# An attention and mixture kernel: row sums out of the value product, bucket numbers per group of queries, a measured bound of the tokens, and a new written order

## The chip, the cores and the metric

The kernel runs on one core of a Trainium2 chip. Its engines are TensorE (PE, with its weight loads apart as PEld), VectorE (DVE), ScalarE (ACT), GpSimd (POOL) and SyncE (SP), which issues most of the DMAs. Each takes its own instructions in their written order and waits at semaphores for the others. The metric is the time of one execution in microseconds (us) on the device; before the change the median of 3 runs is 1019.14 us (1015.75 to 1021.01).

## The reference

Three steps follow each other. `B`, `H`, `S`, `D` are 2, 8, 768, 64; the 1536 tokens have 512 numbers each.

```python
# attention: a query sees only the keys in its own hash bucket (6 sign bits)
q_bucket = sum_over_bits((q @ proj > 0) * 2**bit);  k_bucket likewise
scores = where(q_bucket == k_bucket, q @ k.T / sqrt(D), -1e9)
attn = exp(scores - max(scores));  attn = attn / (sum(attn) + 1e-9);  x = attn @ v
# 4 experts of 512 -> 1024 -> 512, weighted by normalized domain_probs
x = sum over e of p[:, e] * (relu(x @ w1[e]) @ w2[e])
# one more layer 512 -> 2048 -> 512, with a piecewise quadratic activation
out = g(x @ w_in) @ w_out
```

## The kernel before

All products keep about twice the precision of their operands: an operand is split into a high and a low half ("h", "l"), and three matmuls (high by high, high by low, low by high) take the place of one.

**Attention in units.** A unit is one head and 128 queries, against all 768 keys; there are 96. Twelve groups m of units (three blocks of queries by four pairs of heads) have a preparation `prep(m)` each: q, k and v are loaded, their size is bounded, they are split into halves and transposed by DMA, and the keys' bucket numbers are worked out (`kb`). The first block has the queries of two token tiles (16 units), the second four (32), the third six (48). Unit t then goes through these steps:

- `scores` (PE, L636): four matmuls into a PSUM tile `s` of two banks; two of them have 390 columns, the last six of which are the queries' sign bits, since six columns of projections stand behind the keys.
- `q_bucket` (DVE, L646): six bits to a bucket number, with a sum over the six.
- `mask` (DVE, L652): -2**80 where the key's bucket is another. It needs the bucket number.
- `row_max` (DVE, L658): mask added, the result to the tile `e` (three buffers), with the row's minimum.
- `norm` (ACT, L666): the minimum plus 9.704, that is 14 powers of two.
- `expo` (ACT, L671): exp in place, with the row's sum as a second output.
- `p_hi` (ACT, L678), `p_lo` (DVE or POOL, L686, in pieces): the two halves `pn`.
- `p_t` (SP, L691): both are transposed by DMA into `pt`.
- `rsum` (DVE, L696 for each unit, L698 for two units at once): one over (sum plus a small number) times a scale.
- `av`, five units later (PE, L706, L707 and L709, 18 matmuls of 64 columns): the product with the values. From the 17th unit on it is written into free columns of the PSUM tile `s` that the unit five later uses for its scores.
- `comb` (ACT, L716): times the reciprocal, into the token's row of `acc`.

There are two PSUM tiles `s`, so the scores of unit t+2 wait until the tile is read out: by `row_max` of unit t and by `comb` of unit t-5.

**Filling work.** The first token tiles are ready when the 16th unit is combined. Then jobs of the experts run in TensorE's gaps: `JOBS_A`, 19 jobs of 256 tokens by 512 hidden columns each. A job has 48 matmuls of 256 columns (L850 to L852) and 24 of 512 (L868 to L870). ACT writes the high half of weights (L832) and of the hidden layer (L857), DVE or POOL the low halves (L836, L862), and DVE adds the results to `acc` (L880). Before the first job each of two tiles is transposed (L779). Where nothing is to do, unneeded matmuls of zeros (L1040) are written into TensorE's list.

**The order** of all this is fixed when the kernel is built. A planner (`Order`) gets every step with the engines that may do it, a cost, what it reads and writes, and a key. It goes through the steps as a list: of those that can start first it takes the one of the smallest key. The keys are times in units plus a table of numbers (`K_LD` to `K_L2`). Where a step may run on two engines, the planner's costs choose.

**Second phase.** What follows (`step`, `l1b`, `l2b`) is written by hand: the rest of the experts and the last layer, in 16-bit halves. There tokens are scaled by a power of two, bounded in `x_bound` (L1261 to L1267) from the sizes of v.

Of the kernel before, what the change touches and what calls it, by code (L numbers as in the profile page):

```python
# [19 lines left out]
NB = 6  # L20
# [5 lines left out]
LSHIFT = 9.70406052783923  # L26
EPS = 1e-9 * 2.0 ** 14
# [259 lines left out]
def attn_moe_kernel(ctx: ExitStack, tc, q, k, v, proj, probs, w1, w2, w_in, w_out, out):  # L287
# [23 lines left out]
    const.tile([128, 80], F32, name="pad")  # L311
# [20 lines left out]
            vs=kv_p.tile([128, 2, 6, 128], F16, name=f"vs{p}"),  # L332
# [54 lines left out]
    def all_max(nm, n, src, key, r, use, e_out, s_out, w_e, w_s, tag="mx"):  # L387

        st, gb, gc, bm = {}, S.bank(), S.bank(), S.buf(tag, 4)

        def f1():
            st["mx"] = sm_p.tile([4, 1], F32, tag=tag, name=tag)
            st["dg"] = sm_p.tile([4, 4], BF16, tag="d" + tag, name="d" + tag)
            dve.tensor_reduce(st["mx"][0:n], gb.ps[0:n, 0:128], AX.X, ALU.max)
# [25 lines left out]
    sw_b = const.tile([128, 2], F32, name="sw_b")  # L420
    ekv = [const.tile([128, 3], F32, name=f"ekv{i}") for i in range(8)]
    skv = [const.tile([128, 3], F32, name=f"skv{i}") for i in range(8)]

    def prep(m):
# [158 lines left out]
        for i in range(2):  # L583
            tk(f"sw{m}{i}", dict(dve=0.07 + 0.067 * n, sp=0.55), lambda e, i=i: q_swap(i, e), max(t - Q_SW[g], dh + 1.5), r=[f"xq{m}"], w=[f"yq{m}{i}"],
               use=[bxq], port=True, dma=(0.46, 0.75, 0.12 * n, 2.5))
        if kv:
            dv = t - V_HI[g]
            tk(f"vhi{m}", dict(act=0.83), lambda e: hi_(vs[:, :, :, 0:64], st["rv"], 1), dv, r=[vt, f"s{m}.1"] + va, w=[f"vsh{p}"], use=bv)
            tk(f"vlo{m}", dict(dve=0.93), lambda e: lo_(vs[:, :, :, 64:128], vs[:, :, :, 0:64], st["rv"], 1), dv + 0.4,
# [27 lines left out]
    K_LD, V_LD, Q_LD = (17.214, -0.655, 23.922), (12.706, 49.119, 26.44), (12.617, -7.397, 30.338)  # L617
    K_AB, V_AB, Q_AB = (49.192, 45.359, 12.84), (11.282, -23.228, 13.919), (13.718, 15.385, -1.48)
    K_HI, V_HI, Q_HI = (32.317, -13.974, 10.395), (7.816, 1.17, -30.115), (14.167, 8.304, 9.444)
    K_M = 1.18  # L620
    K_NA = 0.604
    K_BI, Q_SW = (2.317, -33.361, 20.951), (10.382, -5.64, -40.487)
# [7 lines left out]
    def scores(t):  # L630
        m, hh, c = units[t]
        st = P[m]
        sps = s_tile(t)
        for j, n in ((1, 390), (0, 384)):
            for i in range(2):
                pe.matmul(sps[:, j, 0:n], st["xq"][1 - i][:, hh * QG[pgs[m][0]][2] + c], st["x"][:, hh, 384 * j:384 * j + n],  # L636
                          start=(i == 0), stop=(i == 1))

    def q_bucket(t):
        u = U[t]  # L640
        if "sm2" not in u:
            s2 = sm_p.tile([128, 6, 2], F32, tag="usm", bufs=6, name="usm")
            U[t ^ 1]["sm2"] = u["sm2"] = s2
        sm = u["sm"] = u["sm2"][:, :, t % 2]
        junk = sm_p.tile([128, NB], F32, tag="junk", bufs=2, name="junk")
        dve.scalar_tensor_tensor(junk, u["s"][:, 1, 384:390], 0.0, pow6, ALU.is_gt, ALU.mult, accum_out=sm[:, 0:1])  # L646

    def mask(t):
# [3 lines left out]
        dve.tensor_scalar(mk, P[m]["kb"][:, hh], u["sm"][:, 0:1], -BIG, ALU.not_equal, ALU.mult)  # L652

    def row_max(t):
        m, hh, c = units[t]
        u = U[t]
        e = u["e"] = e_p.tile([128, 768], F32, tag="e", name="e")
# [35 lines left out]
    def rsum(t, i):  # L693
        s2 = U[t]["sm2"]
        if i < 2:
            dve.tensor_scalar(s2[:, 4, i:i + 1], s2[:, 3, i:i + 1], EPS, P[units[t][0]]["kvs"][:, 1:2], ALU.add, ALU.mult)  # L696
        else:
            dve.reciprocal(s2[:, 5], s2[:, 4])  # L698

    def av(t, gb):  # L700
# [3 lines left out]
        o = u["av"] = s_tile(t + AVL + 1)[:, 0, 384:448] if gb is None else gb.ps[:, 0:64]  # L704
        for i in range(6):
            pe.matmul(o, u["pt"][:, i], vs[:, hh, i, 0:64], start=(i == 0), stop=False)  # L706
            pe.matmul(o, u["pt"][:, i], vs[:, hh, i, 64:128], start=False, stop=False)  # L707
        for i in range(6):
            pe.matmul(o, u["pt"][:, 6 + i], vs[:, hh, i, 0:64], start=False, stop=(i == 5))  # L709

    def comb(t):
# [11 lines left out]
    def unit(t):  # L723
# [17 lines left out]
        if on:  # L741
# [3 lines left out]
            kvm = m - 4 if pgs[m][0] == 1 else m  # L745
# [3 lines left out]
            tk(f"sc{t}", dict(pe=0.66), lambda e: scores(t), t - 1 + K_SC, r=[f"xq{m}", f"yq{m}0", f"yq{m}1", f"x{p}{hh}", "xk6"], after=["bits01"] if t == 0 else [],  # L749
               w=[f"sco{t}"], use=[bS[t], st["bxq"]], excl=ex)  # L750
            tk(f"qb{t}", dict(dve=0.075), lambda e: q_bucket(t), t, r=[f"sco{t}"], w=[f"sm0.{t}"], use=[bS[t], bU[t]], excl=ex, tick=t)
            tk(f"mk{t}", dict(dve=0.329), lambda e: mask(t), t + 0.05, r=[f"sm0.{t}", f"kb{p}{hh}0", f"kb{p}{hh}1"], w=[f"mk{t}"], use=[bmk, bU[t]], port=True)
            tk(f"rm{t}", dict(dve=0.94), lambda e: row_max(t), t + 0.1, r=[f"sco{t}", f"mk{t}", f"sc{m}"], w=[f"e{t}", f"sm1.{t}"],
               use=[be, bS[t], bmk, st["bsc"], bU[t]], excl=ex)
            tk(f"nm{t}", dict(act=0.095), lambda e: norm(t), t + 0.2, r=[f"sm1.{t}"], w=[f"sm2.{t}"], use=[bU[t]])
# [742 lines left out]
```

## Time and profile before

The profiled execution took 1019.93 us, and the span from its first to its last instruction is 1018.1 us.

| | before |
|---|---|
| median of 3 runs | 1019.14 us |
| profiled execution, its span | 1019.93 us, 1018.1 us |
| busy: PE, PEld | 963.4 us (95%), 619.1 us (61%) |
| busy: DVE, ACT, POOL | 731.4 us (72%), 732.2 us (72%), 353.8 us (35%) |
| mean granted clock of TensorE | 0.979 of full speed |
| DMA | 121.51 MB, mean 119 GB/s |

Three stretches are to be told apart. Up to 89 us there are attention units and preparations only. Then, until the first matmul of the second phase at 430.66 us, units and jobs share the engines. The rest is the second phase. Busy time of an engine counts each instruction from its start to its end. TensorE's matmuls overlap, and small instructions on DVE and ACT overlap the next by some 0.07 us; what one costs its engine is therefore read from the distance between two starts.

### The profile page before, as it was taken

How to read it: one execution, taken by the hardware profiler on the slowest of the kernel's cores; microseconds unless marked ns; L12 is line 12 of the kernel's file. 1: busy time of each engine (PE TensorE's matmuls, PEld its weight loads, DVE VectorE, ACT ScalarE, POOL GpSimd, SP SyncE). 2: the span in 40 equal slices, each digit the busy share in tenths (PEclk: the TensorE clock that was granted, in tenths of full speed). 3: DMA queues.
4: the chain of work that ended last, by engine and by line, in shares of the span. 5: the costliest groups of instructions: out<-in, count | busy, mean ns of one | idle time of the engine just before them, and what ended most of it. 6: DMA issues, size and time to landing. Idle time of an engine off the chain costs nothing.

```text
span 1018.1 us, 19428 instructions
## 1 busy us (share of the span) xinstructions
PE 963.4 (95%) x6874; PEld 619.1 (61%) x6874; DVE 731.4 (72%) x1946; ACT 732.2 (72%) x1590; POOL 353.8 (35%) x382
## 2 busy tenths in 40 slices
PE   6668999989999999999999999999998999999998
PEld 2347777868787888875555555555544555555553
DVE  6899978898887886446666657565577678774654
ACT  6888978888887877348776777667776785656442
POOL 0433545544554545515110111104242353434221
PEclk7789999999999999999999999999999999999999
DMA  8899999998999977261434333110110111100002
GB/s 227 191 204 197 199 239 217 251 211 165 233 191 177 195 160 161 81 220 42 146 88 141 103 111 118 42 42 22 43 42 21 43 42 43 41 1 1 1 36 90
DMA packets 254836, 121.51 MB, mean 119 GB/s; under 512 B 180753, under 2 KB 239505, under 8 KB 254737
## 3 DMA queue, kind: packets, MB, share of 16 engines
q1 hardware_dynamic: 251904, 117.89, 49.4%
q10 hardware_dynamic: 2832, 2.36, 0.8%
q8 instruction: 54, 0.88, 0.4%
q14 instruction: 46, 0.37, 0.1%
HBM read 70.28 MB, written 3.15 MB: 72 GB/s over the span
## 4 chain that ended last, share of the span: by engine, by line
PE 62%; DVE 14%; ACT 10%; DMA 9%; issue 4%; SPq 1%; POOL 1%; DVEq 0%; ACTq 0%; POOLq 0%
PE mm L1334 7%; PE mm L1335 7%; PE mm L1336 7%; PE o L1370 6%; PE o L1372 6%; PE o L1371 6%; DMA raw<-in_moe_w_dram 5%; PE s L636 3%; DVE hl L1358 2%; PE m L868 2%; PE m L850 2%; PE m L870 2%; PE m L851 2%; PE m L869 2%; PE m L852 2%
## 5 line engine op out<-in xcount | busy, mean ns | idle before, releaser
L686 POOL TENSOR_TENSOR pn<-e,pn 128x192 f16<-128x192 f32 (+3 forms) x146 | 127.3, 877 | 185.0 <-DVE pn L686 56.6
L1353 POOL TENSOR_TENSOR gg<-gg,ga 128x384 f32<-128x384 f32 x64 | 71.0, 1109 | 153.0 <-DVE ga L1352 142.6
L1343 DVE TENSOR_TENSOR hl<-gg,hh 128x384 f16<-128x384 f32 x72 | 42.9, 595 | 81.3 <-ACT hh L1342 81.1
L658 DVE CUSTOM_DVE_ANT_0 e<-s,mk,sc 128x768 f32<-128x768 f32 x96 | 96.7, 1009 | 3.8 <-ACT acc L716 2.2
L850 PE MATMUL m<-x0h,w1h 128*128 128x256 f32 x304 | 92.1, 303 | 1.1 <-DVE acc L880 1.1
L1350 ACT ACTIVATE ga<-mm,half,k 128x384 f32<-128x384 f32 x64 | 42.7, 667 | 67.9 <-PE mm L1336 46.7
L636 PE MATMUL s<-xk,xq 128*128 128x384 f16 (+1 forms) x384 | 82.4, 340 | 9.1 <-DVE usm L658 7.6
L671 ACT ACTIVATE e<-e,usm 128x768 f32<-128x768 f32 x96 | 89.3, 930 | 2.5
L851 PE MATMUL m<-x0l,w1h 128*128 128x256 f32 x304 | 86.3, 284 | 0.1
L852 PE MATMUL m<-x0h,w1l 128*128 128x256 f32 x304 | 86.1, 283 | 0.0
L678 ACT ACTIVATE pn<-e 128x768 f16<-128x768 f32 (+3 forms) x118 | 84.3, 715 | 2.2 <-DMA pt<-pn 1.3
L1352 DVE SCALAR_TENSOR_TENSOR ga<-ga 128x384 f32<-128x384 f32 x64 | 38.4, 601 | 63.8 <-ACT ga L1350 63.8
L1372 PE MATMUL o<-w2l,hl 128*128 128x512 f16 x216 | 81.9, 379 | 1.1 <-DVE hl L1358 1.1
L1370 PE MATMUL o<-w2l,hh 128*128 128x512 f16 x216 | 82.0, 380 | 0.0
L1371 PE MATMUL o<-w2l,hh 128*128 128x512 f16 x216 | 81.9, 379 | 0.0
L1358 DVE SCALAR_TENSOR_TENSOR hl<-gg,k,hh 128x384 f16<-128x384 f32 x64 | 58.4, 913 | 20.3 <-ACT hh L1357 20.0
L1370 PE MATMUL o<-w2h,hh 128*128 128x512 f16 x192 | 72.9, 380 | 0.0
L1371 PE MATMUL o<-w2h,hh 128*128 128x512 f16 x192 | 72.8, 379 | 0.0
L1372 PE MATMUL o<-w2h,hl 128*128 128x512 f16 x192 | 72.8, 379 | 0.0
L1372 PEld LDWEIGHTS <-hl 128*128 128x128 f16 x408 | 39.9, 98 | 49.7 <-DVE hl L1358 1.6
L1341 ACT ACTIVATE gg<-mm 128x384 f32<-128x384 f32 x72 | 34.8, 483 | 45.1 <-PE mm L1104 20.9
L868 PE MATMUL m<-w2h,hh 128*128 128x512 f32 x152 | 64.6, 425 | 0.7 <-DVE hl L862 0.7
(258 smaller groups left out, 2953.1 us busy)
## 6 DMA issues: line engine op xcount, KB each, us to landing
raw<-in_moe_w_dram SPq DMA_DIRECT2D x127, 256.0 KB, 3.5
r<-in_moe_w_in_dram SPq DMA_DIRECT2D x16, 512.0 KB, 3.6
r<-in_moe_w_out_dram SPq DMA_DIRECT2D x16, 512.0 KB, 3.6
rawx<-in_moe_w_dram SPq DMA_DIRECT2D x24, 256.0 KB, 4.4
out_dram<-acc SPq DMA_DIRECT2D x12, 256.0 KB, 2.0
raw<-in_moe_w_dram ACTq DMA_DIRECT2D x9, 256.0 KB, 3.5
w<-in_moe_w_dram SPq DMA_DIRECT2D x8, 256.0 KB, 6.2
rk<-in_k_dram SPq DMA_DIRECT2D x5, 384.0 KB, 4.1
```

The source lines that it names most:

```text
L636: pe.matmul(sps[:, j, 0:n], st["xq"][1 - i][:, hh * QG[pgs[m][0]][2] + c], st["x"][:, hh, 384 * j:384 * j + n], start=(i == 0), stop=(i == 1))
L658: dve.tensor_tensor_reduce(out=e.rearrange("p (a b) -> p a b", a=2), in0=u["s"][:, :, 0:384], in1=u["mk"].rearrange("p (a b) -> p a b", a= ...
L671: act.activation(u["e"], u["e"], AF.Exp, scale=-1.0, bias=sm[:, 2:3], accum_out=sm[:, 3:4])
L678: act.activation(u["pn"][:, c0:c1], u["e"][:, c0:c1], AF.Copy)
L686: eng[e].tensor_tensor(u["pn"][:, 768 + c0:768 + c1], u["e"][:, c0:c1], u["pn"][:, c0:c1], ALU.subtract)
L850: pe.matmul(ps[:, 0:n], hi[:, ws], xh[:, kc, xs], start=(kc == 0), stop=False)
L851: pe.matmul(ps[:, 0:n], hi[:, ws], xl[:, kc, xs], start=False, stop=False)
L852: pe.matmul(ps[:, 0:n], lo[:, ws], xh[:, kc, xs], start=False, stop=(kc == KC - 1))
L868: pe.matmul(o, hh[:, ts], whi, start=(f == 0), stop=False)
L1370: pe.matmul(o, hh[:, ts], whi, start=(f == 0), stop=False)
L1371: pe.matmul(o, hh[:, ts], wlo, start=False, stop=False)
L1372: pe.matmul(o, hl[:, ts], whi, start=False, stop=(f == 3))
```

## The change

- A column of ones is put beside the values, so `av` gives the row sum as a 65th column; exp no longer sums. `rsum` is now done after `av`, for each unit, out of PSUM. `comb` may run on DVE as well as ACT.
- The bias of exp is the row minimum itself; `norm` goes.
- The queries' bits are no longer columns of the scores. For each group a step `q_bits` makes them with two matmuls of 6 columns for each unit of the group, and two DVE instructions make all bucket numbers of the group. `mask` then needs no scores.
- The tokens' bound of the second phase is measured: a sum of absolute values over each of the 12 tiles of `acc` (DVE or ACT), a maximum, and the chain that other bounds have too. `x_bound` goes.
- The table of numbers is another, so the planner writes another order.

```diff
@@ prep
+        def q_bits():
+            for i in range(2 * n):
+                for z in range(2):
+                    pe.matmul(gq.ps[:, NB * i:NB * i + NB], st["xq"][1 - z][:, i], x[:, i // n, 768:774], start=(z == 0), stop=(z == 1))
+        def q_bucket(i):
+            if i == 0:
+                st["jq"] = sm_p.tile([128, 12, NB], F32, tag="jq", bufs=1, name="jq")
+                dve.scalar_tensor_tensor(st["jq"][:, 0:2 * n], gq.ps[...], 0.0, pow6..., ALU.is_gt, ALU.mult)
+            else:
+                st["qb"] = sm_p.tile([128, 12], F32, tag="qb", bufs=2, name="qb")
+                dve.tensor_reduce(st["qb"][:, 0:2 * n], st["jq"][:, 0:2 * n], AX.X, ALU.add)
+        tk(f"qbp{m}", dict(pe=0.12 * n), lambda e: q_bits(), dq, r=[f"xq{m}", f"yq{m}0", f"yq{m}1", "xk6"], w=[f"qbp{m}"], use=[bxq], grp=gq)
...
@@ table of numbers (two of its lines)
-    K_AV, K_SC, K_CB, K_HI_, K_LO_ = -10.443, -1.424, 0.486, 1.113, 2.995
+    K_AV, K_SC, K_CB, K_HI_, K_LO_ = -101.924, 32.319, 1.164, -27.484, 2.38
@@ a unit
-        for j, n in ((1, 390), (0, 384)):
+        for j in (1, 0):
-        dve.scalar_tensor_tensor(junk, u["s"][:, 1, 384:390], 0.0, pow6, ALU.is_gt, ALU.mult, accum_out=sm[:, 0:1])
-        dve.tensor_scalar(mk, P[m]["kb"][:, hh], u["sm"][:, 0:1], -BIG, ALU.not_equal, ALU.mult)
+        dve.tensor_scalar(mk, P[m]["kb"][:, hh], P[m]["qb"][:, i:i + 1], -BIG, ALU.not_equal, ALU.mult)
-        act.activation(sm[:, 2:3], sm[:, 1:2], AF.Copy, bias=LSHIFT)
-        act.activation(u["e"], u["e"], AF.Exp, scale=-1.0, bias=sm[:, 2:3], accum_out=sm[:, 3:4])
+        act.activation(u["e"], u["e"], AF.Exp, scale=-1.0, bias=u["sm"][:, 0:1])
-            dve.tensor_scalar(s2[:, 4, i:i + 1], s2[:, 3, i:i + 1], EPS, P[units[t][0]]["kvs"][:, 1:2], ALU.add, ALU.mult)
-            dve.reciprocal(s2[:, 5], s2[:, 4])
+            dve.tensor_scalar(sm[:, 1:2], u["av"][:, 64:65], EPS, P[units[t][0]]["kvs"][:, 1:2], ALU.add, ALU.mult)
+            dve.reciprocal(sm[:, 2:3], sm[:, 1:2])
-            pe.matmul(o, u["pt"][:, i], vs[:, hh, i, 0:64], start=(i == 0), stop=False)
+            pe.matmul(o, u["pt"][:, i], vs[:, hh, i, 0:65], start=(i == 0), stop=False)
-        act.activation(acc[TT0[g] + c][:, hd * 64:hd * 64 + 64], u["av"], AF.Copy, scale=u["sm"][:, 5:6])
+        if e == "act":
+            act.activation(to, u["av"][:, 0:64], AF.Copy, scale=sc)
+        else:
+            dve.tensor_scalar(to, u["av"][:, 0:64], sc, None, ALU.mult)
...
-            tk(f"cb{a}", dict(act=0.2), lambda e: comb(a), a + da + K_CB, r=[f"av{a}", f"sm5.{a // 2}"], w=a_of(tt), grp=gb,
+            tk(f"rs{a}", dict(dve=0.12), lambda e: rsum(a, 0), a + da + K_CB - 0.2, r=[f"av{a}", f"s{kvm}.1"], w=[f"sm4.{a}"], grp=gb, **ub)
+            tk(f"rr{a}", dict(dve=0.08), lambda e: rsum(a, 1), a + da + K_CB - 0.1, r=[f"sm4.{a}"], w=[f"sm5.{a}"], use=[bU[a]])
+            tk(f"cb{a}", dict(act=0.2, dve=0.15), lambda e: comb(a, e), a + da + K_CB, r=[f"av{a}", f"sm5.{a}"], w=a_of(tt), grp=gb, **ub)
@@ bound of the tokens
+        def x_scan(e, tt):
+            if e == "dve":
+                dve.tensor_reduce(am_x[:, tt:tt + 1], acc[tt], AX.X, ALU.add, apply_absolute_value=True)
+            else:
+                junk = nat_p.tile([128, 768], BF16, tag="ja", name="ja")[:, 0:512]
+                act.activation(junk, acc[tt], AF.Abs, accum_out=am_x[:, tt:tt + 1])
...
-            dve.tensor_tensor(e, v[0], v[1], ALU.add)
-            ...
-        for b in range(2):
-            x_bound(b)
+        dve.tensor_scalar(exk, ex, 2.0 ** 15, None, ALU.mult)
```

In the written order of the changed kernel 69 of the 96 combinations stand on DVE and 27 on ACT; before all 96 stood on ACT. The low halves of `pn` are 45 pieces on DVE (before 87) and 160 on POOL (before 146, smaller ones). Of the 12 scans of tokens 8 stand on DVE, and 28 weight loads are issued on ACT's queue (before 9).

On DVE, around the `row_max` of the 62nd unit, this stood before (`junk` is the bits times powers of two, `usm` a unit's small numbers, `mk` the mask, `pn` and `w2l` low halves):

```order
L646 SCALAR_TENSOR_TENSOR junk,usm<-s,pow_109 128x6
L836 TENSOR_TENSOR w2l<-raw_3825,w2h 128x256
L652 TENSOR_SCALAR mk<-kb_124,usm 128x768
L686 TENSOR_TENSOR pn<-e,pn 128x192
L836 TENSOR_TENSOR w2l<-raw_3836,w2h 128x256
L658 ISA e,usm<-s,mk,sc 128x768
L658 ISA usm 128x1
L696 TENSOR_SCALAR usm<-usm,skv_149 128x1
```

Around the same `row_max` this stands now (`qb` holds the group's bucket numbers):

```order
L717 TENSOR_SCALAR usm<-s,skv_152 128x1
L683 ISA e,usm<-s,mk,sc 128x768
L683 ISA usm 128x1
L719 RECIPROCAL usm<-usm 128x1
L533 TENSOR_SCALAR sc<-sc 128x1
L741 TENSOR_SCALAR acc<-s,usm 128x64
```

The test of bits is gone from between the scores and the mask. A first instruction of `rsum` that reads `av`'s columns of the tile `s` stands ahead of `row_max`, and reciprocal and combination stand behind it.

On ACT, around the exp of the same unit, this stood before (`hh` is the hidden layer's high half, `w2h` that of weights):

```order
L666 ACTIVATE usm<-usm 128x1
L820 DMA raw_4804<-in_moe_w_dram 128x512
L832 ACTIVATE w2h<-raw_4742 128x512
L671 ACTIVATE e,usm<-e,usm 128x768
L857 ACTIVATE hh<-m 128x256
L678 ACTIVATE pn<-e 128x768
```

And now, from the next exp on:

```order
L691 ACTIVATE e<-e,usm 128x768
L854 ACTIVATE w1h<-raw_4793 128x512
L879 ACTIVATE hh<-m 128x256
L698 ACTIVATE pn<-e 128x768
L838 DMA raw_5216<-in_moe_w_dram 128x4x128
```

The step `norm` no longer stands ahead of exp, and exp writes `e` alone.

On PE, where the queries of a new group (the last pair of heads, third block) come in, scores were followed by a job's matmuls:

```order
L636 LDWEIGHTS xq_5462
L636 MATMUL s<-xk_129,xq_5462 128x390
L636 LDWEIGHTS xq_5461
L636 MATMUL s<-xk_129,xq_5461 128x390
L636 LDWEIGHTS xq_5462
L636 MATMUL s<-xk_129,xq_5462 128x384
L636 LDWEIGHTS xq_5461
L636 MATMUL s<-xk_129,xq_5461 128x384
L868 MATMUL m<-w2h,hh 128x512
```

Now 24 pairs like the last two follow the scores of the unit before (`xq_5801`, `xq_5802` are the new group's queries):

```order
L661 LDWEIGHTS xq_4992
L661 MATMUL s<-xk_126,xq_4992 128x384
L594 LDWEIGHTS xq_5802
L594 MATMUL m<-xk_129,xq_5802 128x6
L594 LDWEIGHTS xq_5801
L594 MATMUL m<-xk_129,xq_5801 128x6
```

The two wide matmuls lose six columns, and each pair of narrow ones brings a weight load of its own. There are 192 narrow matmuls in all, 32 of them for the first block.

## Rows read from the trace of the kernel before

**Rows 1.** Windows: PE, PEld, DVE, ACT, POOL busy (instructions), PEclk, DMA share, GB/s.

```profile
0.00:89.00 89.00, 61.50 (x519) 33.85 (x520) 75.36 (x305) 71.92 (x169) 21.40 (x29) 0.81 0.92 207
89.00:430.60 341.60, 329.33 (x3233) 274.76 (x3231) 279.19 (x868) 272.43 (x646) 169.39 (x211) 1.00 0.92 191
442.00:1018.10 576.10, 563.78 (x3068) 301.86 (x3066) 372.40 (x757) 385.28 (x770) 158.69 (x136) 1.00 0.19 59
```

**Rows 2.** PE's groups, 89 to 430.6 us: count | busy, mean ns | idle before.

```profile
L850 PE MATMUL m<-x0h,w1h 128*128 128x256 f32 x304 | 92.1, 303 | 1.1 <-DVE acc L880 1.1
...
L868 PE MATMUL m<-w2h,hh 128*128 128x512 f32 x152 | 64.6, 425 | 0.7 <-DVE hl L862 0.7
L636 PE MATMUL s<-xk,xq 128*128 128x390 f16 (+1 forms) x300 | 62.2, 330 | 0.0
...
L706 PE MATMUL s<-vs,pt 128*128 128x64 f16 x450 | 37.4, 195 | 5.4 <-DMA pt<-pn 3.3 <-DVE usm L696 1.6 <-DVE junk L646 0.5
```

**Rows 3.** PE in order of time: start, us, line, what, count.

```profile
203.09 0.39 PE L870 MATMUL m<-w2h,hl 128*128 128x512 f32 x1
203.32 0.20 PE L706 MATMUL s<-vs,pt 128*128 128x64 f16 x1
...
203.68 0.34 PE L709 MATMUL s<-vs,pt 128*128 128x64 f16 x6
```

**Rows 4.** The same, a job's first layer a little later.

```profile
205.19 0.28 PE L850 MATMUL m<-x0h,w1h 128*128 128x256 f32 x1
205.31 0.28 PE L851 MATMUL m<-x0l,w1h 128*128 128x256 f32 x1
```

**Rows 5.** The chain of waits, scores of one unit: start, us.

```profile
111.48 0.66 PE s L636 x4
```

**Rows 6.** What PE waited for, 89 to 430.6 us: total, times, longest.

```profile
PE s L706 <- DMA pt<-pn: 3.3, 6, 1.5
PE m L597 <- DMA xk<-nk: 2.2, 3, 1.3
```

**Rows 7.** The first token tile's transposes on PE.

```profile
89.04 0.60 PE L779 MATMUL m<-ident,acc 128*128 128x128 f32 x4
```

**Rows 8.** ACT in order of time, one unit.

```profile
68.87 0.19 ACT L666 ACTIVATE usm<-usm 128x1 f32<-128x1 f32 x1
68.96 0.31 ACT L716 ACTIVATE acc<-m,usm 128x64 f32<-128x64 f32 x1
69.16 0.93 ACT L671 ACTIVATE e<-e,usm 128x768 f32<-128x768 f32 x1
70.00 0.18 ACT L671 ACTIVATION_READ_ACCUMULATOR e<-e,usm 128x1 f32 x1
70.09 0.47 ACT L613 ACTIVATE kb<-m 128x384 bf16<-128x384 f32 x1
```

**Rows 9.** DVE in order of time, one unit.

```profile
203.55 0.20 DVE L696 TENSOR_SCALAR usm<-usm,skv 128x1 f32<-128x1 f32 x1
203.67 0.15 DVE L646 SCALAR_TENSOR_TENSOR junk<-s,pow 128x6 f32<-128x6 f32 x1
...
203.79 0.17 DVE L698 RECIPROCAL usm<-usm 128x2 f32<-128x2 f32 x1
203.87 0.82 DVE L652 TENSOR_SCALAR mk<-kb,usm 128x768 bf16<-128x768 bf16 x1
```

**Rows 10.** DVE's groups by form, 0 to 430.6 us.

```profile
L686 DVE TENSOR_TENSOR pn<-e,pn 128x192 f16<-128x192 f32 x71 | 28.9, 408 | 0.0
...
L824 DVE TENSOR_REDUCE am_w<-raw 128x1 f32<-128x512 f32 x5 | 3.3, 680 | 3.4 <-DMA raw<-in_moe_w_dram 3.3
```

**Rows 11.** PE around a single narrow matmul.

```profile
415.56 0.17 PE L411 MATMUL m<-dmxw,ones 2*128 2x2 bf16 x1
415.66 0.50 PE L868 MATMUL m<-w2h,hh 128*128 128x512 f32 x1
```

**Rows 12.** ACT at the start of the second phase.

```profile
434.89 0.63 ACT L832 ACTIVATE w2h<-raw 128x512 fp32r<-128x512 f32 x1 [0.81 <-DMA raw<-in_moe_w_dram]
```

More of the change, by code (lines that the diff above doesn't have):

```diff
@@ L310, in attn_moe_kernel @@
     ident = const.tile([128, 128], F32, name="ident")
-    const.tile([128, 80], F32, name="pad")
+    const.tile([128, 24], F32, name="pad")
     half = const.tile([128, 1], F32, name="half")
@@ L331, in attn_moe_kernel @@
             kb=kv_p.tile([128, 2, 768], BF16, name=f"kb{p}"),
-            vs=kv_p.tile([128, 2, 6, 128], F16, name=f"vs{p}"),
+            vs=kv_p.tile([128, 1568], F16, name=f"vs{p}")[:, 0:1560].rearrange("p (h c d) -> p h c d", h=2, c=6),
         )
@@ L420, in attn_moe_kernel @@
     sw_b = const.tile([128, 2], F32, name="sw_b")
+    am_x = const.tile([128, 12], F32, name="am_x")
+    mx_x = const.tile([128, 2], F32, name="mx_x")
+    ex = const.tile([128, 2], F32, name="ex")
+    sx = const.tile([128, 2], F32, name="sx")
     ekv = [const.tile([128, 3], F32, name=f"ekv{i}") for i in range(8)]
@@ L656, in row_max @@
         u = U[t]
+        sums(t)
         e = u["e"] = e_p.tile([128, 768], F32, tag="e", name="e")
@@ L951, in fill @@
                    r=[f"l2.{j}.{i}.3", "pr"], w=a_of(tt), grp=gb)
-    K_LDW, K_WHI, K_WLO, K_XT = 2.992, -0.836, -3.345, 20.559
-    K_EVA, K_EVD, K_L2 = 0.084, -7.646, -32.852
+        for tt in range(6, 12):
+            x_bound(tt)
+        tk("mxx", dict(dve=0.15), lambda e: dve.tensor_reduce(mx_x, am_x.rearrange("p (b t) -> p b t", b=2), AX.X, ALU.max), 100,
+           r=[f"amx{i}" for i in range(12)], w=["mxx"])
+        all_max("mxy", 2, lambda: mx_x, 100, ["mxx"], [], lambda: ex, lambda: sx, ["ex"], ["sx"], "mxv")
+    K_XS = -79.736
+    K_LDW, K_WHI, K_WLO, K_XT = -227.274, -8.417, -22.583, -52.671
+    K_EVA, K_EVD, K_L2 = -8.736, -15.304, -25.186
     with tc.manual_schedule():
@@ L966, in attn_moe_kernel @@
             dve.memset(pow6[:, i:i + 1], float(2 ** i))
+        for x in kvs:
+            pool.memset(x["vs"][:, :, :, 64:65], 1.0)
         make_identity(nc, ident)
@@ L1250, in need @@
                     next(w64)
-        ex = const.tile([128, 2], F32, name="ex")
-        sx = const.tile([128, 2], F32, name="sx")
         exk = const.tile([128, 2], F32, name="exk")
@@ L1257, in attn_moe_kernel @@
         prk, k5 = {}, {}
-        def x_bound(b):
-            e, v = ex[:, b:b + 1], [ekv[4 * b + i][:, 1:2] for i in range(4)]
-            dve.tensor_tensor(e, v[0], v[1], ALU.add)
-            dve.tensor_tensor(e, e, v[2], ALU.add)
-            dve.tensor_tensor(e, e, v[3], ALU.add)
-            dve.tensor_scalar(e, e, 4.0, None, ALU.mult)
-            pow2(e)
-            dve.reciprocal(sx[:, b:b + 1], e)
-            dve.tensor_scalar(exk[:, b:b + 1], e, 2.0 ** 15, None, ALU.mult)
         def x_f16(kc, c0, c1):
```

82 lines of the change are left out of this document (43 added, 39 removed).

## The prediction

> **What bounds the kernel now.** I read three views in this order: the windows, to find the stretches with different limits; TensorE's groups and its order in time, for how full its list really is; and its waits.
>
> The windows split the span in three [rows 1]. After 442 us the second phase keeps PE busy for 563.8 of 576.1 us, and the change touches only one DVE step at its start. In the first 89 us PE is busy for 61.5 us, DVE for 75.4 and ACT for 71.9, at a granted clock of 0.81: here the units alone run, and DVE and ACT hand work to each other. This ends when the 16th unit is combined and the first tile's transposes start [rows 7]. From then to 430.6 us PE shows 329.3 of 341.6 us [rows 1]. That busy time counts overlaps, so I add up its list by distances between starts. A matmul of 256 columns takes 0.12 us [rows 4], one of 512 takes 0.23, one of the value product 0.03 (12 starts in 0.36 us) [rows 3], a unit's four scores 0.66 [rows 5]. The counts in this stretch [rows 2] give 3 x 304 x 0.12 = 109.4, 3 x 152 x 0.23 = 104.9, 75 x 0.66 = 49.5, and 81 units of the value product (75 into `s`, 6 elsewhere) x 18 x 0.03 = 43.7 us, together 307.5. The small groups (bucket bits of keys, transposes, filler) add some 15 us, an estimate. So PE's list fills about 322 of 341.6 us, and 19 us are gaps. PE is the bound here, and an engine that gets less work shortens this stretch only by what it takes out of those 19 us. The longest named waits are for the transposed halves (3.3 us) and for transposed keys (2.2 us) [rows 6]; both are DMAs that the change leaves as they are.
>
> So there are three places to win or lose: the first 89 us, PE's list, and PE's gaps.
>
> **The first 89 us.** Up to the first tile's high half, the written order of ACT had 20 `norm`, 19 sums out of exp and 15 combinations; now it has none of the first two and 3 combinations. By distances between starts a `norm` costs 0.09, a sum 0.09 and a combination 0.20 us [rows 8], so 1.8 + 1.7 + 2.4 = 5.9 us go. But one more exp (0.84) and three more sums for preparations of later groups (0.74 each by exp's neighbours) now stand ahead of that point, some 3 us. On DVE 21 bit tests at 0.12 us go [rows 9] (2.5 us), and 8 fewer low-half pieces of about 0.4 us [rows 10] (some 4 us). In return 12 combinations come (1.8 us at 0.15, since no row shows a 64-column one on DVE: it lies between the 0.12 of a small instruction [rows 9] and the 0.33 of one of 192 columns [rows 10]), 12 bucket instructions (1.2), 7 more reciprocals at 0.08 [rows 9], three more copies of queries, one scan, and one more mask and `row_max` (1.3). That leaves about 1 us less. So this stretch gains 1 us if DVE's list decides and 5.9 if ACT's does and the work drawn ahead finds gaps. I take 4, since each unit's chain also loses two steps on ACT between the minimum and the end of exp. For the range I keep a loss of 1 (the later groups' sums delay the first tile) and a gain of 8 (the 5.9, and 2 more if the 79 filler matmuls that stand ahead of the 12th unit's end, before 48, keep the clock up).
>
> **PE's list.** 160 of the 192 narrow matmuls stand after the first block, where PE is full. No row shows a matmul of 6 columns with a full weight load of its own. The nearest is the value product, which has such a load for 64 columns and takes 0.03 us [rows 3]: 160 x 0.03 = 4.8 us. From above, the distance of a lone 2-column matmul to the next is 0.10 us [rows 11], which makes 16 us; from below, if all fall into gaps, nothing. I take 4.8, because they stand in a row of pairs as those of rows 3 do. Six fewer columns in 192 scores and one more in two thirds of the value product are each about half a microsecond and cancel. The 32 narrow ones of the first block have PE's gaps there as cover.
>
> The Trainium skill ("TensorE: Matmul & The Clock Gate", section "Back-to-back issue gap") says that a stream of weight load and matmul pairs is paced by both and sustains about 81 ns per matmul at 128 columns. By it the 160 pairs would cost 13.0 us. The value product's pairs at 30 ns [rows 3] speak against it here; it is the fifth case below.
>
> **PE's gaps.** Over all units ACT loses 96 x (0.09 + 0.09) and 69 combinations x 0.20 [rows 8], 31 us, and gets four scans and 19 DMA issues, some 4 us: it is relieved by about 27 of 344 us [rows 1]. DVE is hardly relieved: 96 tests (11.5 us) and 42 low-half pieces (some 14 us) go, while 69 combinations (10.4), 48 more reciprocals (3.8), 24 bucket instructions (3.6), eight scans at 0.6 [rows 10] (4.8) and seven copies come, so about 1 us less of 354 [rows 1]. POOL takes over the low halves, some 23 us more of 191 [rows 1], and is half idle. What moves is the balance: before the last scores stood 774 first-layer and 381 second-layer matmuls in units of one of the three lines each, now 714 and 336, so attention runs ahead and 60 x 0.12 + 45 x 0.23 = 17.6 us of jobs more follow it, where PE has nothing to wait for but weights. I take 8 of the 19 us of gaps as won; the bounds are nothing (the gaps are DMA's [rows 6]) and 17.
>
> The scans of tokens and their chain are in these sums. The 14 instructions of `x_bound` lay beside matmuls, so their going gains nothing, and what is late there stays: ACT is held by a weight load [rows 12], and the same rows stand in the same order in the changed kernel.
>
> **A wait that is added.** `rsum` now waits on DVE for the value product, which waits for a transpose. Queued behind it are `row_max`, the next mask and low halves; exp waits for the first. The combination, two more DVE steps later, frees the PSUM tile for scores. I price this at nothing in the sum: a tile is used every second unit, that is each 2 x 341.6 / 75 = 9.1 us [rows 1, 2], and PE's scores had no idle time ahead of them in this stretch [rows 2].
>
> **Sum.** 1019.9 (the profiled execution) - 4 + 4.8 - 8 = 1012.7. The median of the runs shown is 0.8 lower, so I predict 1012 us.
>
> **Rivals.**
> - *Forecast*, chance 0.48: 1012, own range 1007 to 1018 (first stretch -1 to -6, gaps -4 to -12).
> - *Relief where nobody waits*, 0.27: the first 89 us gain 4, the list grows by 4.8, and the gaps stay, since they belong to DMAs and to DVE, which is as loaded as before: 1020.7, as a median 1020. For it: rows 6 and DVE's sum. Against it: ACT's 27 us.
> - *The new order closes the gaps*, 0.14: -8 + 4.8 - 17 = -20.2, as a median 999. For it: 13.6 us in which DVE was idle in the first 89 us [rows 1]. Against it: no edit shortens a DMA.
> - *The longer way out of PSUM*, 0.06, slower: `rsum`, a `row_max` of some 0.9 us, a reciprocal and the combination now stand between the value product and the release of `s`, where one ACT instruction of 0.3 us stood [rows 8]. It frees about 1 us later. If PE stands still for that at every fourth of 75 units, 19 us come on top of the forecast: 1031. It decides from the point at which scores follow the release by less than 1 us. Against it: the 9.1 us of a tile's round.
> - *Pairs at 81 ns*, 0.05: 1012 + 160 x 0.051 = 1020, a rival by the rule that the skill's page gives above.
>
> **How the numbers follow.** About 0.5% (5.1 us) is what a measurement of this kernel can tell from no change, so faster is below 1014.0 and slower above 1024.2. The forecast's case gives 0.34 faster and 0.14 same, the second 0.02, 0.22 and 0.03, the third 0.14 faster, the fourth 0.06 slower, the fifth 0.04 same and 0.01 slower: 0.50, 0.40 and 0.10. The range 1000 to 1024 leaves out half of the third case, the fourth, and the upper ends of the second and fifth, some 0.17.
>
> **What would show it.** The first tile's transposes start at about 85 us. The narrow matmuls follow each other at 0.03 us. The first matmul of the second phase starts at about 423 us (430.7 before), and the second phase lasts as long as before. PE's gaps between these points shrink from some 19 to 11 us. The forecast is wrong if the transposes start no earlier than 88 us, if PE waits for the combination ahead of scores, or if POOL's low halves come so late that PE waits for transposed halves for more than the 3.3 us of before.

## The result, and the profile after

The changed kernel is slower: a median of 1029.91 us (4 runs, 1028.64 to 1032.05) beside 1018.74 for the kernel before on the same chip, a ratio of 1.0108 with a 95% interval of 1.0086 to 1.0129. The prediction was 1012, with a range of 1000 to 1024: the measured time lies 18 us above the one and 6 above the other. The profiled execution took 1028.64 us (span 1026.8); the one of before took 1019.93 (span 1018.1). These 8.7 us can be placed by three points in the two traces:

| start of | before | after | added in the stretch |
|---|---|---|---|
| the first tile's transposes | 89.0 | 91.2 | +2.2 |
| the first matmul of the second phase | 430.7 | 437.9 | +5.0 |
| the end | 1018.1 | 1026.8 | +1.5 |

The windows of the changed kernel's trace, cut at these points (columns as in [rows 1]):

```profile
0.00:91.20 91.20, 67.77 (x638) 40.45 (x638) 76.59 (x296) 69.92 (x126) 28.28 (x41) 0.91 0.96 207
91.20:437.90 346.70, 334.76 (x3339) 279.83 (x3335) 280.51 (x807) 243.47 (x424) 181.97 (x215) 0.99 0.92 185
450.00:1026.80 576.80, 563.44 (x3065) 301.42 (x3063) 373.79 (x757) 385.09 (x770) 157.54 (x136) 1.00 0.19 59
```

ACT lost 29 us in the middle stretch (243.5 for 272.4 [rows 1]) and 2 in the first, a little more than the 27 that the prediction counted; DVE stayed as it was and POOL took over some work. Yet the stretch is longer. The DMA share, the last but one number, is the one that hasn't moved: 0.92 in the middle, before and after. It stands in [rows 1] as well. (It adds up the time of all packets over 16 engines, and packets overlap: over the first 330 us of the changed kernel it comes to 1.02. So 1 is not a strict ceiling.)

The groups of PE in the middle stretch answer to [rows 2]:

```profile
L872 PE MATMUL m<-x0h,w1h 128*128 128x256 f32 x304 | 92.4, 304 | 0.0
L890 PE MATMUL m<-w2h,hh 128*128 128x512 f32 x152 | 65.8, 433 | 0.3 <-DVE acc L902 0.3
...
L727 PE MATMUL s<-vs,pt 128*128 128x65 f16 x450 | 39.2, 196 | 4.3 <-DMA pt<-pn 2.3 <-DVE usm L717 1.9
L728 PE MATMUL s<-vs,pt 128*128 128x64 f16 x450 | 38.6, 194 | 0.0
L594 PE MATMUL m<-xk,xq 128*128 128x6 f16 x128 | 4.1, 166 | 2.2 <-DMA xq<-xq 2.2
```

The same count of job matmuls is there, and the narrow ones (L594) are new. Mean durations overlap, so the cost is again read from starts. One value product and one group of narrow matmuls, in order of time:

```profile
114.13 0.54 PE L594 MATMUL m<-xk,xq 128*128 128x6 f16 x16 [0.40 <-DMA xq<-xq]
114.53 0.48 PE L890 MATMUL m<-w2h,hh 128*128 128x512 f32 x1
...
204.92 0.20 PE L727 MATMUL s<-vs,pt 128*128 128x65 f16 x1
204.96 0.20 PE L728 MATMUL s<-vs,pt 128*128 128x64 f16 x1
...
205.31 0.34 PE L730 MATMUL s<-vs,pt 128*128 128x65 f16 x6
```

Sixteen narrow pairs go in 0.40 us, 0.025 each. The first twelve starts of a value product take 0.39 us; in [rows 3] they took 0.36. What PE waited for in the middle stretch (us in total, times, longest), beside [rows 6]:

```profile
PE m L621 <- DMA xk<-nk: 2.4, 1, 2.4
PE s L727 <- DMA pt<-pn: 2.3, 3, 0.9
PE m L594 <- DMA xq<-xq: 2.2, 2, 1.8
PE s L727 <- DVE usm L717: 1.9, 1, 1.9
```

The longest waits are DMAs again. That of L594 is new: the narrow matmuls wait for a copy of the queries. The one for `rsum` (L717) is hardly longer than it was (1.6 us [rows 2]).

TensorE's granted clock has a part in this. Behind the 1.8 us wait of L594, at 188 us, it is at 0.5 of full speed (1.2 GHz) from 191.4 to 194.8 us, and the starts of 256-column matmuls stand 0.21 us apart instead of 0.12:

```profile
191.22 0.40 PE L872 MATMUL m<-x0h,w1h 128*128 128x256 f32 x1
191.43 0.41 PE L873 MATMUL m<-x0l,w1h 128*128 128x256 f32 x1
```

The middle stretch has a second such fall of 3.4 us at 222 us, behind a wait for `kb` at 220; before the change it had one, at 156 us. An estimate from these rows: one more fall costs at most half of its 3.4 us, 1.7 of the 5.0 us that the stretch grew by.

I then took every distance between two starts of PE and set what exceeds the usual distance of its kind (its shape and that of the matmul ahead of it) by more than 0.12 us apart as a gap. From the first tile's transposes to the second phase the gaps are 16.1 us before and 15.9 after: not one of the 8 us that I took is won. The list is longer by about 5. In the first phase as a whole it gained 5.0 us of narrow matmuls, 3.0 of value products (53.7 to 56.7), and 4.5 of zeros, most of which fill gaps of the first 91 us.

### The profile page after: what moved, and what is told of

The parts are those of the page before. It is cut to its first block, busy times and chain, and to the rows that moved or that the text cites. A ratio compares the mean times of both kernels' runs of the same rounds, so it can differ in the third digit from the quotient of the medians.

```text
span 1026.8 us, 19476 instructions
## 1 busy us (share of the span) xinstructions
PE 975.1 (95%) x7095; PEld 630.7 (61%) x7095; DVE 732.5 (71%) x1863; ACT 701.0 (68%) x1325; POOL 372.0 (36%) x396
## 2 busy tenths in 40 slices
DMA packets 254432, 120.89 MB, mean 118 GB/s; under 512 B 180673, under 2 KB 239169, under 8 KB 254337
## 3 DMA queue, kind: packets, MB, share of 16 engines
HBM read 70.28 MB, written 3.15 MB: 72 GB/s over the span
## 4 chain that ended last, share of the span: by engine, by line
PE 65%; DVE 12%; ACT 9%; DMA 8%; issue 3%; POOL 1%; SPq 1%; ACTq 0%; POOLq 0%; DVEq 0%
PE mm L1365 7%; PE mm L1366 7%; PE mm L1367 7%; PE o L1401 6%; PE o L1403 6%; PE o L1402 6%; PE s L661 4%; PE m L872 3%; PE m L873 3%; PE m L874 3%; DMA raw<-in_moe_w_dram 3%; PE m L890 2%; PE m L891 2%; PE m L892 2%; DVE hl L1389 2%
## 5 line engine op out<-in xcount | busy, mean ns | idle before, releaser
L706 POOL TENSOR_TENSOR pn<-e,pn 128x192 f16<-128x192 f32 (+3 forms) x160 | 150.2, 945 | 188.9 <-DVE mk L676 31.6
L661 PE MATMUL s<-xk,xq 128*128 128x384 f16 x384 | 80.7, 334 | 7.1 <-DVE usm L683 4.2
L873 PE MATMUL m<-x0l,w1h 128*128 128x256 f32 x304 | 86.5, 284 | 0.0
L698 ACT ACTIVATE pn<-e 128x768 f16<-128x768 f32 (+3 forms) x104 | 81.0, 787 | 5.9 <-DMA pt<-pn 1.9
```

What stands on the lines that cost most here:

```text
L661: pe.matmul(sps[:, j, 0:384], st["xq"][1 - i][:, hh * QG[pgs[m][0]][2] + c], st["x"][:, hh, 384 * j:384 * j + 384], start=(i == 0), stop=( ...
L698: act.activation(u["pn"][:, c0:c1], u["e"][:, c0:c1], AF.Copy)
L706: eng[e].tensor_tensor(u["pn"][:, 768 + c0:768 + c1], u["e"][:, c0:c1], u["pn"][:, c0:c1], ALU.subtract)
L873: pe.matmul(ps[:, 0:n], hi[:, ws], xl[:, kc, xs], start=False, stop=False)
```

## The experiments

Each ratio is against runs of the kernel before on the same chip, with its 95% interval. "Theory A" is that the change adds to TensorE's list and that its gaps are not ACT's or DVE's; the others are named where they come up. Differences in us are between medians. Unless it is said, the instructions of each engine stand in the same order as in the kernel that was edited, so only their cost differs.

**Relief alone.** The kernel before, without `norm`:

```
 def norm(t):
-    act.activation(sm[:, 2:3], sm[:, 1:2], AF.Copy, bias=LSHIFT)
+    return
```

> The kernel before with the 96 norm steps on ACT left out (exp takes the row minimum itself as its bias), every other instruction in the same place on its engine. One part of the change alone, the one that only removes. Rival C and the prediction (ACT's relief closes TensorE's gaps and shortens the first 89 us): 96 x 0.09 = 8.6 us less on ACT and one step less in each unit's chain, -3 to -5 us, 0.995 to 0.997. Theory A (the gaps are not ACT's): within 1 us, 0.999 to 1.001.

Measured 1.0009 (0.9984 to 1.0035). The same with the bucket tests taken off DVE as well (`mask` compares with `pow6[:, 0:1]`):

> The kernel before without the 96 norm steps on ACT and without the 96 bucket tests on DVE (the mask compares with a constant instead, so the masks are not the reference's), every other instruction in its place. ACT loses 8.6 us and DVE 11.5, more than the whole change relieves DVE by. The prediction's mechanism (relief closes gaps): -6 to -10 us, 0.990 to 0.994. Theory A with D (list, fixed pieces and DMAs): within 2 us, 0.998 to 1.001.

Measured 1.0003 (0.9982 to 1.0025). Its windows, cut at the same two points:

```profile
0.00:87.20 87.20, 60.43 (x519) 34.51 (x520) 73.51 (x261) 69.92 (x149) 21.85 (x29) 0.86 0.92 210
87.20:430.00 342.80, 329.67 (x3233) 276.15 (x3231) 274.30 (x720) 263.78 (x570) 170.23 (x211) 0.99 0.92 191
```

The first tile comes 1.8 us earlier (87.2 for 89.0), and the middle stretch gives back most of it (342.8 for 341.6). Twenty us less of work on ACT and DVE are worth nothing that can be measured, at most 0.2% by the intervals. ACT is relieved here by 8.6 us and not by the 31 of the change, DVE by 11.5; for this much the main term of the prediction is settled: the gaps weren't ACT's or DVE's.

**Whose gaps are they?** The changed kernel with transposes of half the size:

```
-sp.dma_start_transpose(out=u["pt"], in_=u["pn"])
+sp.dma_start_transpose(out=u["pt"][:, 0:6], in_=u["pn"][:, 0:768])
...
-pe.matmul(o, u["pt"][:, 6 + i], vs[:, hh, i, 0:65], ...)
+pe.matmul(o, u["pt"][:, i], vs[:, hh, i, 0:65], ...)
```

> The changed kernel with the transposes of probabilities on the high halves alone (6 pieces instead of 12; the value product takes the high half a second time, so TensorE's list is the same). It leaves the low halves of the probabilities out of the product. Theory D (transposes and loads fill the DMA engines up to 360 us, and the waits that relief cannot close are theirs): the waits of value products for transposes (3.4 and 2.3 us) go, the units run ahead, -5 to -12 us from the changed kernel, 1.000 to 1.006 of the kernel before. Theory A alone (TensorE's list sets the end, its waits are where other work lands): -2 us at most, 1.009 or more.

Measured 0.9898 (0.9875 to 0.9921), 1011.8 us: 18 us below the changed kernel, with the same number of instructions on every engine. And with the transposes whole, but the weights' loads halved:

```
-e.dma_start(t, src[f0:f0 + 128, :])
+e.dma_start(t[:, 0:256], src[f0:f0 + 128, 0:256])
```

> The changed kernel with every expert weight piece of the first phase loaded to half (128 KB instead of 256; engines read the loaded half twice, so their instructions are as many and as long). It leaves half of these weights out. Theory D1 (the DMA engines' time is what is full, whoever uses it): with 17 MB less in the first 360 us the transposes of probabilities land earlier than 4.4 us and the time falls as in the run with half transposes, -8 to -18 us from the changed kernel, 0.993 to 1.004 of the kernel before. Theory D2 (only a transpose's own length counts, in each unit's chain): at most -4 us, 1.007 or more.

Measured 0.9947 (0.9922 to 0.9973), 1015.8 us: 14 us below the changed kernel. The first of the two runs moves 18.9 MB less by DMA (102.02 for 120.89), the second 13.6 MB less (107.26), so each MB is worth about 1 us in both. So it is the DMA engines' time, whoever uses it. The page's row of DMA shows it: the span in 40 slices, each digit the mean busy share of the 16 DMA engines in tenths. Of the kernel before:

```profile
DMA  8899999998999977261434333110110111100002
```

of the changed one:

```profile
DMA  8999999999999886261423244110110111100002
```

and of the run with half transposes:

```profile
DMA  8995889984956753452443333110110111000012
```

A slice is some 25 us, so up to about 330 us the share is 80% or more in every slice, and 90% or more in 10 of the 13 before and 12 of the 13 after. With half transposes it is not: its mean in the middle stretch falls from 0.92 to 0.69, with half loads to 0.83. The waits change too; those of the middle stretch are now, with half transposes:

```profile
PE s L727 <- DVE usm L717: 1.4, 1, 1.4
PE m L621 <- DMA xk<-nk: 1.1, 1, 1.1
PE s L727 <- DMA pt<-pn: 0.6, 2, 0.4
```

The gaps shrink by 9.1 us (by distances, counted on for some 23 us more, to the second phase's first product in 16-bit halves), and the first tile comes at 85.0 us instead of 91.2. With half loads, where the transposes are whole, the gaps shrink by 9.9 us, and of the waits for DMAs named above (6.9 us together) one is left:

```profile
PE m L621 <- DMA xk<-nk: 1.2, 1, 1.2
```

The transposes' landing times (issues, count, median us from issue to landing), here with half transposes:

```profile
pt<-pn SPq DMA_TRANSPOSE x96, 3.7
xk<-nk SPq DMA_TRANSPOSE x16, 3.6
```

and in the changed kernel:

```profile
pt<-pn SPq DMA_TRANSPOSE x96, 4.4
xk<-nk SPq DMA_TRANSPOSE x16, 3.5
```

and with half loads:

```profile
pt<-pn SPq DMA_TRANSPOSE x96, 4.2
xk<-nk SPq DMA_TRANSPOSE x16, 3.1
```

Half transposes shorten their own landing and not that of the keys; half loads bring both kinds in earlier by 0.2 to 0.4 us, though their size is as before. A median hides the long ones. The chain of waits of the changed kernel passes through three transposes ahead of the first tile (start, us); DVE and ACT have other work meanwhile, which is not on this chain:

```profile
45.91 5.48 DMA pt<-pn
...
57.73 4.35 DMA xk<-nk
...
74.86 4.96 DMA xq<-nq
```

The Trainium skill ("Perfetto Trace Analysis", section "Identifying the Most-Contended Engine") advises judging DMA by its use of HBM and not by its occupancy, since sixteen engines make that misleading, and then looking for the DMA resource that binds. By the page of the profile HBM moves 72 GB/s over the span, beside 118 that the DMA engines move, so the first half of this advice by itself misses the transposes. Here occupancy pointed the right way: transposes from SBUF to SBUF aren't in the HBM figure (it stays at 70.28 MB read when 18.9 MB of them go), and the two runs above show that their time counts.

**Does the change pay where transposes are short?** The kernel before, with the same half transposes:

> The kernel before with transposes of the high halves alone (as in the same run of the changed kernel; it leaves the low halves out). Theory R (relief of ACT and POOL's low halves bring something once the transposes are short): the kernel before gains less than the changed one's 18 us, so it ends above 1012 us, 0.993 or more. Theory A (the change only adds, and both are bound by the same DMAs): it gains as much, 1002 us, 0.980 to 0.985.

Measured 0.9842 (0.9806 to 0.9878), 1006.3 us. It gains 1.6% where the changed kernel gained 2.1%, so it falls between the two theories. The changed kernel with half transposes stands at 0.9898: the change costs 5.5 us there too, but that is half of what it costs with whole ones. The traces place the difference. Behind the first tile the change is dearer by about as much as ever: 336.1 for 330.3 us up to the second phase, of which 4.5 are list. Ahead of it the change now wins: the first tile comes at 85.0 for 86.9 us, where with whole transposes it came 2.2 us late. So relief (or the new order; the two aren't told apart) is worth some 2 us in the first stretch once transposes are short, and nothing in the middle one.

**What the list costs.** Row sums out of exp again, values in the old layout:

```
-act.activation(u["e"], u["e"], AF.Exp, scale=-1.0, bias=u["sm"][:, 0:1])
+act.activation(u["e"], u["e"], AF.Exp, scale=-1.0, bias=u["sm"][:, 0:1], accum_out=u["sm"][:, 1:2])
...
-vs=kv_p.tile([128, 1568], F16, ...)[:, 0:1560].rearrange("p (h c d) -> p h c d", h=2, c=6)
+vs=kv_p.tile([128, 2, 6, 128], F16, ...)
```

> The changed kernel with the row sums taken out of exp again (accumulated by ACT, read where the 65th column was read) and the value product on 64 columns in the old layout; order kept. In the changed kernel's trace the value product takes 56.7 us by distances between starts against 53.7 before. Theory A (list): -3.1 us, 1.008 of the kernel before, although ACT gets 96 x 0.09 = 8.6 us of work back. Rival C (ACT's relief is worth something): the 8.6 us on ACT cost more than the 3.1 bring, 1.011 or more.

Measured 1.0044 (1.0025 to 1.0063), 1024.8 us: 5 us better than the changed kernel, although ACT gets its 8.6 us back. Is it the 65th column, or where the operand stands? With ACT's sums and 64 columns, but 130 elements per chunk:

> Row sums out of exp as in the run with ACT's sums, 64 columns in every matmul of the value product, but the values stay in the changed kernel's layout (130 elements per key chunk instead of 128); order kept. If the place of the operand in SBUF is what slowed the value product: its matmuls take 0.032 to 0.034 us as in the changed kernel, 1.007 to 1.010 of the kernel before. If the 65th column did it: 0.029 to 0.030 us, and the time of the run with ACT's sums, 1.004.

Measured 1.0096 (1.0066 to 1.0125). Its starts in a value product,

```profile
209.44 0.19 PE L728 MATMUL s<-vs,pt 128*128 128x64 f16 x1
...
209.78 0.34 PE L730 MATMUL s<-vs,pt 128*128 128x64 f16 x6
```

and those of the run with the old layout:

```profile
206.59 0.19 PE L728 MATMUL s<-vs,pt 128*128 128x64 f16 x1
...
206.91 0.34 PE L730 MATMUL s<-vs,pt 128*128 128x64 f16 x6
```

From the second to the thirteenth start it takes 0.34 us in the one and 0.32 in the other. Over all units the median distance in the old layout is 0.029 us at every place behind the first; in the shifted one it swings between 0.028 and 0.034 with the place of the chunk. That is some 3 us of list; the 65th column adds some 1.5, which the times (1.0096 and 1.0108) don't show. So the 5 us come from the layout, not from the column.

The narrow matmuls, cut to 24 (two for each of the twelve groups; the recorded expectation counts 32) and doubled to 384:

```
-for i in range(2 * n):
-    for z in range(2):
-        pe.matmul(gq.ps[:, NB * i:NB * i + NB], st["xq"][1 - z][:, i], x[:, i // n, 768:774], ...)
+for z in range(2):
+    pe.matmul(gq.ps[:, 0:NB * 2 * n], st["xq"][1 - z][:, 0], x[:, 0:1, 768:774].to_broadcast([128, 2 * n, NB]), ...)
```

> The changed kernel with its 192 narrow matmuls (6 columns, a weight load each) cut to 32, two per group of queries; order and everything else stay. It leaves out the bucket bits of all query tiles but the first of a group, so the masks are not the reference's. Theory A (TensorE's list is what grew): in the changed kernel's trace the 192 take 5.0 us by distances between starts and 3.1 us of waits stand ahead of them; 160 fewer take 4.1 us of list away, so 1.0115 - 0.004 = about 1.007 of the kernel before (1026), and down to 1.004 if their waits go too. Rival B (they lie in gaps, the loss is in the order): no difference from the changed kernel, 1.011.

> The changed kernel with every narrow matmul issued twice (384; the bits keep their signs), order kept. Theory A: + 192 x 0.026 = 5.0 us, 1.016 of the kernel before (1035). Rival B: within 1 us of the changed kernel, 1.011 to 1.012.

Measured 1.0144 (1.0114 to 1.0174) with 24 and 1.0106 (1.0072 to 1.014) with 384, so theory A failed for them: neither fewer nor more makes a difference in the expected direction. With 24 the list is shorter by 3.6 us and the gaps longer by 5.6; at 322 us both that run and the changed kernel wait for the same transposed keys. What PE saves ahead of such a wait is lost in it. That the run with 24 came out at the upper end is, in its profiled execution, a matter of the second phase, which the edit doesn't touch: it starts at 438.4 us for 437.9, but takes 593.3 us for 588.8, at a mean granted clock of 0.988 for 0.997.

**A false trail.** In all traces the first 32-bit matmul behind a unit's scores stands 0.253 us ahead of the next instead of 0.12. I took this for the price of changing from 16-bit to 32-bit operands, some 9 us in all. Two runs tested it. One inserts 2-column matmuls of zeros into first-layer blocks of the changed kernel:

```
+if kc == 2:
+    pe.matmul(ps[:, 0:2], warm[:, 0:128], warm[:, 0:2], start=False, stop=False)
 pe.matmul(ps[:, 0:n], hi[:, ws], xh[:, kc, xs], start=(kc == 0), stop=False)
```

> The changed kernel with 84 more matmuls: ahead of the third inner slice of each first-layer block stands one 2-column bf16 matmul that adds zeros to the block's PSUM tile; order kept. Theory S (a change of TensorE from 16-bit to 32-bit operands costs a fixed piece, which is most of what the prediction took for gaps): the first 32-bit matmul behind each inserted one takes 0.20 us to the next instead of 0.12, as it does behind value products in both traces, so 84 x (0.03 + 0.08) = 9 us of list, and +5 to +9 us in time (part may vanish in waits): 1.016 to 1.020 of the kernel before. Rival (those 0.08 to 0.13 us belong to what PE waits for there): 84 x 0.03 = 2.5 us, 1.011 to 1.014.

Measured 1.0173 (1.0141 to 1.0205). Its trace, at one inserted matmul (L873):

```profile
379.98 0.28 PE L876 MATMUL m<-x0h,w1l 128*128 128x256 f32 x1
380.10 0.18 PE L873 MATMUL m<-warm 128*128 128x2 bf16 x1
380.14 0.36 PE L874 MATMUL m<-x0h,w1h 128*128 128x256 f32 x1
380.34 0.28 PE L875 MATMUL m<-x0l,w1h 128*128 128x256 f32 x1
```

It takes 0.04 us, and 0.20 pass behind it instead of 0.12: a 2-column matmul between 32-bit ones costs 0.12. The other run exchanges scores and value product where they follow each other:

> The kernel before with one exchange on TensorE: where a value product is followed at once by a unit's scores, the scores now stand first (75 places; row_max then waits for the value product, as it waited for the scores). In both traces the first 32-bit matmul behind scores takes 0.253 us to the next instead of 0.12, behind a value product 0.20. Theory S (that piece depends on the 16-bit work just ahead): 63 such places x 0.05 = 3.2 us less list and 0.995 to 0.999 in time, less what the later row_max takes back. Rival (the piece belongs to the waits of the first-layer blocks): no difference, 0.999 to 1.002.

> The same exchange (75 places) in the changed kernel with ACT's sums and the old layout of values. Theory S: 3 us below that run's 1.0044, so 1.001 to 1.004. Rival: 1.004 to 1.006.

Measured 1.0027 (1.0007 to 1.0048) and 1.0062 (1.0039 to 1.0085), no gain in either. The exchanged places show why (in the kernel before with the exchange):

```profile
264.59 0.83 PE L652 MATMUL s<-xk,xq 128*128 128x390 f16 x4
265.25 0.19 PE L722 MATMUL s<-vs,pt 128*128 128x64 f16 x1
...
265.78 0.47 PE L884 MATMUL m<-w2h,hh 128*128 128x512 f32 x1
```

Four scores take 0.66 us when a value product follows. When a job follows, the last of them shows only 0.03 to the next start, and the missing 0.13 appear behind the job's first matmul. They belong to the score, and nothing is lost there. Behind small 16-bit matmuls the 0.08 are real, but that happens at some 20 to 30 places only.

**The order.** In two runs the planner draws the order anew: the changed kernel with the numbers of the kernel before, and the changed kernel with combinations on ACT alone (`dict(act=0.2)`).

> The changed kernel ordered by the numbers of the kernel before (queries' bucket bits due 2 units ahead, scans of tokens 20 units behind). Theory D (the new order is what loses: its first key transposes and unit chains come late): 1.000 to 1.006 of the kernel before. Theory A (the new instructions lose, whatever their order): 1.010 or more; numbers fitted to other instructions may also cost a few us more, up to 1.02.

> The changed kernel with all combinations on ACT, as before; the planner draws the order anew. Theory E (work shifted to DVE slows the units' chain): DVE loses some 81 combinations x 0.15 = 12 us and the first tile's transposes start 2 us earlier, 1.006 to 1.009. Theory A: DVE's load isn't what sets the end, 1.009 to 1.013.

Measured 1.0172 (1.014 to 1.0204) and 1.0197 (1.0163 to 1.0231). Both are worse than the changed kernel, and neither decides its question: numbers fitted to one set of steps place another set badly. In the second one PE's waits for transposes are three times what [rows 6] show, and here PE does wait for the combination:

```profile
PE s L727 <- DMA pt<-pn: 10.7, 11, 2.7
...
PE s L727 <- ACT acc L739: 3.5, 4, 1.3
```

So the new table suits the new steps better than the old one does. Whether part of the loss is the new order's is not shown: another fitted table was not tried, nor the old order with the new instructions in it.

**A faster version** joins the two things that helped, half transposes and the old layout of values with ACT's sums, and drops the third group of the value product. It is less exact, so it isn't a like for like replacement:

```
-for i in range(6):
-    pe.matmul(o, u["pt"][:, 6 + i], vs[:, hh, i, 0:64], start=False, stop=(i == 5))
```

> The changed kernel with ACT's sums and the old layout of values, with half transposes, and without the third group of the value product: the probabilities enter it as their 16-bit high half alone (less exact; POOL still writes the low halves, which nobody reads). TensorE's list is 96 x 6 x 0.03 = 17 us shorter, of which some 10 stand behind the first tile. Theories A and D together: the run with half transposes (0.990), 5 us less for the layout, and up to 10 of the list: 0.975 to 0.985. If the DMAs alone set the pace: 0.985 to 0.990.

Measured 0.9798 (0.976 to 0.9836), 1002.2 us, below both kernels. The kernel before with the same third group dropped was not run; with half transposes alone it stands at 0.9842, so this run doesn't show that the change itself pays.

## Why the prediction was wrong

- **What bounds the middle stretch.** The prediction said that PE's list fills 322 of 341.6 us and that 19 us are gaps. Both were about right (16 us by distances). It also said that the longest named waits are DMAs that the change leaves as they are. The conclusion drawn from this was wrong.
- **The step that failed: "I take 8 of the 19 us of gaps as won".** Nothing was won, 16.1 to 15.9 us. The step priced relief of ACT by what ACT lost, while the waits named DMAs. The runs without `norm` and without bucket tests show relief worth at most 0.2%, and the two light-DMA runs show that 9 to 10 us of gaps go with DMA time. The second case, "Relief where nobody waits", had the mechanism, though not the size.
- **The first 89 us: -4 predicted, +2.2 measured.** It is the same mistake. Units 4 to 8 come 6 to 11 us earlier (`row_max` of unit 6 starts at 37.8 us for 44.3), but unit 12 is where it was (69.6 for 69.5), because the transposes of keys, queries and probabilities that stand in the chain above fall into full DMA engines. With half transposes unit 12 starts its `row_max` at 63.6, and the first tile comes 1.9 us ahead of that of the kernel before with half transposes: half of the gain that was forecast. Of the prediction's own signs of being wrong this one came: the transposes started no earlier than 88 us. Why the first tile is 2 us later rather than equal was not isolated; the order of the loads is new too.
- **PE's list: the narrow matmuls.** 4.8 us were predicted for 160 of them at 0.03; all 192 took 5.0, at 0.026. The 81 ns of the fifth case didn't show. Only 128 stand behind the first tile's transposes, not 160. But taking them out brought nothing: the list's term isn't the time's term where PE waits for transposed keys behind them. Their wait for the queries' copies (2.2 us) was not in the sum.
- **PE's list: the value product.** "One more column in two thirds of the value product" was put at half a microsecond. Its list grew by 3.0 us, mostly through the layout of the values that came with the column, and undoing it brought 5. This is the largest part of the loss that one edit accounts for. The remaining 0.44% (4.5 us) no single edit accounts for; its cause stays open.
- **The added wait** was priced at nothing, rightly for the middle stretch: PE waits once for `rsum` (1.9 us, before 1.6) and not for the combination ahead of scores. "The longer way out of PSUM" landed on about the measured time, by a mechanism that the changed kernel doesn't show.
- **The second phase** was to last as long as before and took 1.5 us more in the profiled execution (588.8 for 587.5). Its length differs by more than that between executions of the same second phase: the kernel before without `norm` has 591.7, at a mean granted clock of 0.991 for 0.996. So these 1.5 us can't be put down to the change.

By its own terms: the second case's 1020.7, with +2.2 for -4 and 3.0 for the values, makes 1029.9 for the 1028.6 of the profiled execution. That is an account along PE and partly luck, since the narrow matmuls in it are not worth their 4.8 and the second phase's 1.5 are left out.

## What to carry to other kernels

Before an edit is credited with closing gaps, look at what ends them; if it is DMA, read the DMA engines' busy share of that stretch, and where it is high (0.92 here) credit nothing to relief of other engines before a run has shown it. Two runs settle it cheaply: one that leaves out the work to be saved, with the order unchanged, and one that halves the transfers. An extra column in a small matmul is cheap by itself, but look at where it moves the operands that follow it.

## What the runs showed of the hardware

- In a stream of value products, a 64-column f16 matmul takes 0.029 us where the values lie in chunks of 128 elements. Where the chunks are 130 elements apart it takes 0.028 to 0.034, by the place of the chunk; the changed kernel, with a 65th column in two of three, shows 0.029 to 0.035.
- A 2-column bf16 matmul between 32-bit ones costs 0.12 us (0.04 and 0.08 behind it).
- A 6-column f16 pair of weight load and matmul takes 0.025 us in a row of 16.
- Distances between starts in the trace can put a matmul's time on the one behind it: the last of a unit's scores shows 0.03 us to the start of a 32-bit matmul, whose own distance is then 0.13 us longer, while ahead of a value product it shows 0.16.
- Transposes from SBUF to SBUF fill the DMA engines without showing in the HBM bytes: with 18.9 MB of them less, the middle stretch's DMA share fell from 0.92 to 0.69, and HBM read stayed at 70.28 MB.
